# Six q tiles turned in 32x32 squares through DRAM on VectorE, and the routing table's lane one-hots as Sign steps on ScalarE

## The chip, the cores and the metric

The kernel runs on one core of a Trainium2 chip. A core has a matrix engine (TensorE), three engines for elementwise work (VectorE, ScalarE, GpSimd), a queue engine that issues DMAs (SyncE), an on-chip memory of 128 partitions and a small accumulator memory (PSUM) into which TensorE writes. Each engine works through its own instructions in the order in which the program gives them and waits on semaphores for the others. The metric is the device time of one execution in microseconds (us); less is better.

## What is computed

The kernel adds three things: the input x, a linear attention block, and a mixture of experts, both on the normalised x. S = 2048 tokens, D = 512, 32 heads of 16, 8 experts of which each token takes two, with 1792 hidden units. Cut to what matters here:

```python
def _A_ref(x, wqkv, wo):
    q, k, v = qkv[0], qkv[1], qkv[2]              # (b, heads, s, 16)
    phi = lambda t: jnp.where(t > 0, t + 1, jnp.exp(t)) + 1e-6
    pq, pk = phi(q), phi(k)
    kv = jnp.einsum("bhsd,bhse->bhde", pk, v)
    z = jnp.einsum("bhsd->bhd", pk)
    num = jnp.einsum("bhqd,bhde->bhqe", pq, kv)
    den = jnp.einsum("bhqd,bhd->bhq", pq, z)[..., None] + 1e-6
    return (num / den).transpose(...).reshape(B, S, D) @ wo

def _B_ref(x, w_gate, w1, w2):
    topk_idx = jnp.argsort(-(xf @ w_gate), axis=-1)[:, :2]
    gates = softmax(topk_val)
    for e in range(8):
        out = out + w_e * (silu(xf @ w1[e]) @ w2[e])   # w_e: the token's gate for e, or 0

xn = _layernorm(x)
return x + _A_ref(xn, A_wqkv, A_wo) + _B_ref(xn, B_w_gate, B_w1, B_w2)
```

## The kernel before

Tokens are tiled by 128: 16 tiles. Products keep nearly full precision by splitting each operand into a high part (rounded by a ScalarE copy, `split_hi`, L141) and a low part (the rest, a VectorE subtraction, `split_lo`, L144), and adding three products (high by high, high by low, low by high). The order of all work is written out by hand from the line `tc.manual_schedule()` on: each engine executes its steps in the order in which the code calls them. Buffers come from pools with a fixed number of slots per tag: `ta` (tag "a", 11 slots), `um` and `tb` (tag "u", 20), `sm` (tag "s", 18), and the accumulator tags "acc" (4), "mm" (2) and "tr" (2).

The kernel has three stages. The first normalises x, projects k and gathers two sums over all tokens; from them comes one matrix M (512x512), held in high and low parts, which merges kv with wo. The second, the q loop (L1531), goes over the q tiles t: here the change lies. The third runs the experts, from about 194 us on; in it the last five q tiles are finished too.

One iteration t of the q loop issues, in this order:

- `o_out(t-4)`: VectorE adds the finished attention output to x (L1478), SyncE stores it;
- side steps: the generator `side_jobs` gives VectorE a piece of the routing (which token goes to which place of which expert) worth some 2.6 us. In iterations 7 to 10 the piece is `table(q)`, q = 0 to 3 (L639): it builds, for 512 assignments (token and choice), a lane one-hot (`ohl`, 128 places in a block, L645) and a block one-hot multiplied by the token number (`mvb`, L647, L650). The products of the one-hots, `table_mm(q)` (L655), add up to the table of tokens by place. In iteration 11 `table_end` (L663) makes index lists of it, with which GpSimd gathers the rows of the first expert (`gather1`);
- `q_den(t-1)`: VectorE sums z-weighted features to denominators (L1410);
- `fetch_w` in iterations 8 to 10: SyncE issues the first three expert weight loads;
- `q_proj(t)`: TensorE's twelve matmuls of q (L1376) into an accumulator bank, then `q_exp(t)`, three ScalarE steps (L1385 to L1387);
- the `late` steps of the iteration before, `table_mm` among them (the last one, `table_mm(3)`, at the end of iteration 10);
- `q_norm(t-1)`: VectorE makes the reciprocals (L1414, L1415), GpSimd multiplies (L1416);
- `q_feat(t)`: VectorE makes the features (`q_phi`, L1393), GpSimd multiplies them by z (L1397);
- `load_x(t-2)`: SyncE fetches x for a later `o_out`;
- `q_transp(t-2)`: TensorE turns the normalised tile by four 128x128 transposes into an accumulator bank (L1422), ScalarE makes the high part and VectorE the low part of the result, `pqT`;
- from iteration 11 on `plain_w`: high and low parts of the first expert's weights;
- `o_proj(t-3)`: TensorE's twelve matmuls of `pqT` with M (L1437).

For the last five tiles (NO = 11 to 15) another way is in place: `pz_out` stores the normalised tile to DRAM as it is, `pz_in` fetches it late in the third stage by four DMAs of 32 partitions each, so that 32-row groups land on the partitions where they are wanted, and `q_turn` transposes it in 32x32 squares, two VectorE instructions of 128x256 (L1454). `q_hi` and `q_lo` make the two parts.

## Time and profile before

| what | value |
|---|---|
| time, median of 3 runs | 826.91 us (826.82 to 826.97) |
| the profiled execution | 826.48 us |
| its span, first to last instruction | 824.8 us |
| granted TensorE clock | 1.00 throughout |
| VectorE busy | 679.6 us (82%) |
| ScalarE busy | 541.2 us (66%) |
| TensorE from o_proj(0) at 123.2 us to the first expert matmul | 70.6 us |

The profile is of one execution. Its times are microseconds from the first instruction; PE is TensorE's matmul row, PEld its weight loads, DVE VectorE, ACT ScalarE, POOL GpSimd, SPq and ACTq the queues from which SyncE and ScalarE issue DMAs. L1376 is line 1376 of the kernel before. In the view of instructions in order of time a row has start, duration, engine, line, operation, output and inputs, shape, count (consecutive like instructions are merged), and in brackets the idle time just before with the instruction that ended it. A matmul's duration includes its way through the array, so matmuls overlap: their rate is read from starts.

### The profile page before, as it was taken

The numbers are of one execution on the slowest core, as the hardware profiler recorded it, in microseconds if no ns is written. First come the engines' busy times: TensorE is split into PE (matmuls) and PEld (weight loads), VectorE is DVE, ScalarE is ACT, GpSimd is POOL, SyncE is SP. The second block draws the span as 40 slices with busy tenths as digits, with TensorE's granted clock in tenths as the row PEclk, the third lists the DMA queues.
The fourth block names the chain that finished last, engine by engine and source line by source line (L and its number), as shares of the span: only waits on it lengthen the run. The fifth ranks groups of instructions, "written<-read, shape, count | busy, mean of one in ns | idle before, by whom it ended". The sixth has DMA issues, their size and how long they took to land. (4 is left out here: it accounts for less than half of the span.)

```text
span 824.8 us, 15897 instructions
## 1 busy us (share of the span) xinstructions
PE 820.3 (99%) x5361; PEld 752.1 (91%) x5361; DVE 679.6 (82%) x1470; ACT 541.2 (66%) x1162; POOL 249.7 (30%) x335
## 2 busy tenths in 40 slices
PE   9999999999999999999999999999999999999998
PEld 8999888889999999999999999999999888888886
DVE  7788889999878887878888788789888987887851
ACT  5575364358666768766876777677768766776650
POOL 5543224375310136121803250443127030012002
PEclk9999999999999999999999999999999999999999
DMA  5752136354764565566557464756576573249507
GB/s 168 252 199 87 52 135 202 128 183 166 234 200 135 152 197 108 145 166 184 131 136 187 151 143 136 206 130 161 155 190 130 161 188 113 84 132 232 154 1 178
DMA packets 106874, 127.69 MB, mean 155 GB/s; under 512 B 15198, under 2 KB 69854, under 8 KB 106758
## 3 DMA queue, kind: packets, MB, share of 16 engines
q1 hardware_dynamic: 92902, 106.43, 42.7%
q0 software_dynamic: 12880, 18.66, 11.8%
q10 hardware_dynamic: 1008, 1.57, 0.5%
q8 instruction: 43, 0.70, 0.3%
q14 instruction: 41, 0.34, 0.1%
HBM read 93.95 MB, written 31.09 MB: 152 GB/s over the span
## 5 line engine op out<-in xcount | busy, mean ns | idle before, releaser
L1174 POOL DMA_INDIRECT out_dram<-yo,sidx x22 | 35.1, 1595 | 282.6 <-DVE yo L1169 260.4
L1174 POOL DMA_INDIRECT out_dram<-yu,L x47 | 78.0, 1659 | 85.9 <-ACT yu L1267 59.0
L144 DVE TENSOR_TENSOR h<-hs,h 128x576 fp32r<-128x576 f32 (+7 forms) x112 | 77.7, 694 | 5.7 <-ACT h L141 5.4
L141 ACT ACTIVATE h<-hs 128x576 fp32r<-128x576 f32 (+7 forms) x112 | 72.3, 646 | 3.2
L1324 ACT ACTIVATE hs<-px 128x276 f32<-128x276 f32 (+7 forms) x54 | 21.1, 390 | 58.7 <-PE px L1316 58.6
L1339 ACT ACTIVATE hs<-hs 128x276 f32<-128x276 f32 (+7 forms) x54 | 23.0, 426 | 46.5 <-DVE hs L1338 46.5
L1338 DVE TENSOR_TENSOR hs<-pz,hs 128x276 f32<-128x276 f32 (+7 forms) x54 | 23.3, 431 | 34.6 <-PE pz L1316 34.0
L1343 DVE TENSOR_TENSOR hs<-px,hs 128x276 f32<-128x276 f32 (+7 forms) x54 | 23.3, 432 | 33.7 <-PE px L1316 33.7
L1047 POOL DMA_INDIRECT xg<-xn_d,gidx x37 | 40.8, 1104 | 28.2 <-DMA xq<-xs_d 7.2
L437 PE MATMUL gacc<-pkhl,xnhl 128*128 128x512 f32 x192 | 47.9, 397 | 0.0
L437 PEld LDWEIGHTS gacc<-pkhl,xnhl 128*128 128x128 f32 x192 | 34.8, 188 | 6.8
L1173 POOL MEMSET spacer<- 1x1 f32 x69 | 38.4, 557 | 6.8 <-DVE ws_3l L144 6.8
L1349 DVE TENSOR_TENSOR hs<-py,hs 128x276 f32<-128x276 f32 (+7 forms) x54 | 23.0, 426 | 13.7 <-PE py L1316 13.4
L1344 ACT ACTIVATE hs<-hs 128x276 f32<-128x276 f32 (+7 forms) x54 | 22.8, 422 | 17.0 <-DVE hs L1343 15.8
L411 POOL TENSOR_TENSOR zz<-zz,pk 128x512 f32<-128x512 f32 x14 | 18.2, 1300 | 48.3 <-DVE L L404 48.3
L1385 ACT ACTIVATE e_q<-qp 128x512 f32<-128x512 f32 x16 | 9.6, 598 | 35.4 <-PE qp L1376 31.7
L1198 PE MATMUL y<-w_1h,h 128*128 128x512 f32 (+2 forms) x88 | 32.0, 394 | 0.0
L1198 PE MATMUL y<-w_5h,h 128*128 128x512 f32 (+2 forms) x88 | 32.0, 394 | 0.0
L1198 PE MATMUL y<-w_2h,h 128*128 128x512 f32 (+2 forms) x88 | 32.0, 393 | 0.0
L1198 PE MATMUL y<-w_3h,h 128*128 128x512 f32 (+2 forms) x88 | 32.0, 393 | 0.0
L1198 PE MATMUL y<-w_0h,h 128*128 128x512 f32 (+2 forms) x88 | 32.0, 393 | 0.0
L1198 PE MATMUL y<-w_4h,h 128*128 128x512 f32 (+2 forms) x88 | 31.7, 393 | 0.0
(563 smaller groups left out, 3152.8 us busy)
## 6 DMA issues: line engine op xcount, KB each, us to landing
wst<-in_B_w_dram SPq DMA_DIRECT2D x196, 128.0 KB
wst<-in_B_w_dram SPq DMA_DIRECT2D x37, 512.0 KB
zz<-in_B_w_dram SPq DMA_DIRECT2D x26, 512.0 KB
xs_d<-xg SPq DMA_DIRECT2D x117, 64.0 KB
xq<-xs_d SPq DMA_DIRECT2D x28, 256.0 KB
x<-in_A_x_dram SPq DMA_DIRECT2D x27, 256.0 KB
xn_d<-xn SPq DMA_DIRECT2D x16, 256.0 KB
xnT<-xn SPq DMA_DIRECT2D x11, 256.0 KB
```

The costliest lines, as they stand in the source:

```text
L141: A.activation(hi, src, AF.Copy)
L144: V.tensor_tensor(lo, src, raw(hi), op=ALU.subtract)
L437: T.matmul(gacc[d], xnhl[:, a, d * P:(d + 1) * P], pkhl[:, b, :], start=(t == 0 and i == 0), stop=(t == NT - 1 and i == 2))
L1047: G.indirect_dma_start(out=raw(t), out_offset=None, in_=xn_d, in_offset=IOA(ap=gidx[:, b:b + 1], axis=0))
L1173: G.memset(spacer, 0.0)
L1174: st = G.indirect_dma_start(out=rows, out_offset=IOA(ap=idx, axis=0), in_=src, in_offset=None, compute_op=ALU.add).ins
L1198: T.matmul(ya[r, d][:m], h[a][:, d * P:d * P + m], w[b][:, n % 2, :], start=(first and i == 0), stop=(last and i == 2))
L1338: V.tensor_tensor(c12, pz_, c12, op=ALU.add)
L1339: A.activation(c12, c12, AF.Silu)
L1343: V.tensor_tensor(c22, px, c22, op=ALU.add)
L1344: A.activation(c22, c22, AF.Silu)
L1349: V.tensor_tensor(c11, pz_, c11, op=ALU.add)
```

## The change

It has two parts, and a third that follows from the second.

Tiles 4 to 9 (`TURNED`) are no longer transposed on TensorE. `q_norm` writes such a tile with its columns regrouped (the 32-column groups of each quarter put together); in the next iteration `pz_out` stores it to DRAM right behind `q_norm`, and `pz_in` fetches it back by the four DMAs of 32 partitions, after `load_x`. One iteration later `q_turn`, `q_hi` and `q_lo` take the place of `q_transp`. The fetched and the turned tile lie in the two halves of one "u" buffer, the two parts in an "s" buffer as before.

The lane one-hot of `table(q)` was one VectorE comparison of 128x1024. Now ScalarE makes eight instructions of 128x128, each sign(lane - (i + 0.5)) for one column of assignments, with the lane as bias: +1 for the places i below the lane and -1 from the lane on, a step instead of a one-hot. The lanes are held in 4 bytes for that.

The products then give sums of steps, and the table is the difference of neighbouring rows, halved. So `table_steps` builds a difference matrix on GpSimd (in iteration 8), `table_split` splits the sums into a high part (ScalarE) and a low part (VectorE) at the end of iteration 10, and `table_diff` multiplies them by the matrix, two small matmuls, in the middle of `q_proj(11)`. `table_end` runs behind that, after `q_den(10)`, not ahead of it.

```diff
@@ -45,6 +45,7 @@
 PASSES = ((0, 0), (0, 1), (1, 0))
 ND = 5
 NO = NT - ND
+TURNED = range(4, NO - 1)
 NE = 12
 NP = NF // 2
 NPLAIN = 2
@@ -110,6 +111,7 @@
     M_d = tc.dram_tile((2, 2, P, SW), F32, name="M_d")
     pz_d = tc.dram_tile((ND * P, D), F32, name="pz_d")
     xs_d = tc.dram_tile((E * RB * P, D), F32, name="xs_d")
+    pq_d = tc.dram_tile((len(TURNED) * P, D), F32, name="pq_d")
     gate_d = tc.dram_tile((E, BLK, P), F32, name="gate_d")
     sx_d = tc.dram_tile((P, BLK), F32, name="sx_d")
 
@@ -238,6 +240,7 @@
         G.affine_select(out=bmask, in_=bmask, pattern=[[DH, 8], [0, DH]],
                         compare_op=ALU.is_ge, fill=0.0, base=DH - 1, channel_multiplier=-1)
         iota(i_lane, [[1, P]])
+        G.tensor_scalar(i_lane, i_lane, 0.5, None, op0=ALU.add)
         iota(i_blk, [[1, NB]])
         iota(i_ov, [[1, NOV]])
         iota(i_e8, [[0, NT], [1, E]], base=-E)
@@ -441,7 +444,7 @@
 
 
     rt = cst
-    lane_f = rt.tile([P, NT, 2], F16, name="lane_f")
+    lane_f = rt.tile([P, NT, 2], F32, name="lane_f")
     blk_f = rt.tile([P, NT, 2], F16, name="blk_f")
     ohr = rt.tile([P, E, E], F32, name="ohr")
     gate = rt.tile([P, OV0], F32, name="gate")
@@ -640,10 +643,10 @@
         ts = slice(4 * q, 4 * q + 4)
         ohl = ta(f"ohl{q}", 8 * P, F16).rearrange("p (a b) -> p a b", a=8)
         mvb = ta(f"mvb{q}", 8 * NB, F16).rearrange("p (a b) -> p a b", a=8)
-        la = lane_f[:, ts, :].rearrange("p t k -> p (t k)").unsqueeze(2)
+        la = lane_f[:, ts, :].rearrange("p t k -> p (t k)")
         bl = blk_f[:, ts, :].rearrange("p t k -> p (t k)").unsqueeze(2)
-        V.tensor_tensor(ohl, i_lane.unsqueeze(1).broadcast_to([P, 8, P]),
-                        la.broadcast_to([P, 8, P]), op=ALU.is_equal)
+        for i in range(8):
+            A.activation(ohl[:, i, :], i_lane, AF.Sign, bias=la[:, i:i + 1], scale=-1.0)
         V.tensor_tensor(mvb, i_blk.unsqueeze(1).broadcast_to([P, 8, NB]),
                         bl.broadcast_to([P, 8, NB]), op=ALU.is_equal)
         m4 = mvb.rearrange("p (t k) b -> p t (k b)", k=2)
@@ -651,6 +654,14 @@
         tabm[q] = (ohl, mvb)
 
     tabm = {}
+
+    def table_steps():
+        step, tabp[2] = ta("step", P), um("step_r")[:, :P]
+        G.memset(step, 0.0)
+        for base, v in ((0, -0.5), (-1, 0.5), (P - 1, -0.5)):
+            G.affine_select(out=step, in_=step, pattern=[[1, P]], compare_op=ALU.not_equal,
+                            fill=v, base=base, channel_multiplier=-1)
+        G.tensor_copy(tabp[2], step)
 
     def table_mm(q):
         if q == 0:
@@ -660,8 +671,18 @@
             T.matmul(tabp[0], ohl[:, i, :], mvb[:, i, :],
                      start=(q == 0 and i == 0), stop=(q == 3 and i == 7))
 
+    def table_split():
+        tab = wp.tile([P, 2, NB], F32, tag="tab", name="tab", bufs=1)
+        hl = um("tabhl")
+        tabp[1] = tab, hl[:, :NB], hl[:, NB:2 * NB]
+        split(*tabp[1][1:], tabp[0])
+
+    def table_diff():
+        for i in range(2):
+            T.matmul(tabp[0], tabp[2], tabp[1][1 + i], start=(i == 0), stop=(i == 1))
+
     def table_end():
-        tab = wp.tile([P, 2, NB], F32, tag="tab", name="tab", bufs=1)
+        tab = tabp[1][0]
         t1, em = tab[:, 0, :], tab[:, 1, :]
         V.tensor_copy(t1, tabp[0])
         V.tensor_scalar(gidx, t1, -1.0, 0.0, op0=ALU.add, op1=ALU.max)
@@ -677,9 +698,10 @@
         yield from routing()
         for q in range(4):
             table(q)
+            if q == 1:
+                table_steps()
             late.append(lambda q=q: table_mm(q))
             yield 9.0
-        table_end()
 
     marks = []
     side = side_jobs()
@@ -1365,13 +1387,15 @@
         Q.dma_start(out[S + i * P:S + (i + n) * P, :].rearrange("(a p) d -> p a d", p=P),
                     zt.unsqueeze(1).broadcast_to([P, n, D]))
 
-    pq, pz, pqT = {}, {}, {}
+    pq, pz, pzt, pqT = {}, {}, {}, {}
 
     eq = {}
 
-    def q_proj(t, act=True):
+    def q_proj(t, act=True, mid=None):
         qp = psm("mm", f"qp{t}")
         for kc in range(KC):
+            if mid and kc == 2:
+                mid()
             for i, (a, b) in enumerate(PASSES):
                 T.matmul(qp, xT(t, a, kc), wq_v[kc // 2][b][:, kc % 2, :],
                          start=(kc == 0 and i == 0), stop=(kc == KC - 1 and i == 2))
@@ -1413,8 +1437,11 @@
         den = dens.pop(t)
         V.tensor_scalar(den, den, 1e-6, None, op0=ALU.add)
         V.reciprocal(den, den)
-        G.tensor_tensor(heads(pz[t]), heads(pq[t]),
-                        den.unsqueeze(2).broadcast_to([P, H, DH]), op=ALU.mult)
+        out, src, den = heads(pz[t]), heads(pq[t]), den.unsqueeze(2).broadcast_to([P, H, DH])
+        if t in TURNED:
+            out = pz[t].rearrange("p (a k h d) -> p k a h d", a=4, k=KC, d=DH)
+            src, den = (ap.rearrange("p (k a h) d -> p k a h d", a=4, k=KC) for ap in (src, den))
+        G.tensor_tensor(out, src, den, op=ALU.mult)
 
     def q_transp(t):
         p = psm("tr", f"pqp{t}")
@@ -1437,24 +1464,32 @@
                     T.matmul(op, pqT[t][:, a, kc * P:(kc + 1) * P], M_v[kc // 2][b][:, kc % 2, cols],
                              start=(kc == 0 and i == 0), stop=(kc == KC - 1 and i == 2))
 
+    def rows_d(t):
+        return pq_d[(t - TURNED[0]) * P:(t - TURNED[0] + 1) * P, :] if t in TURNED else \
+            pz_d[(t - NO) * P:(t - NO + 1) * P, :]
+
     def pz_out(t):
-        Q.dma_start(pz_d[(t - NO) * P:(t - NO + 1) * P, :], pz.pop(t))
+        Q.dma_start(rows_d(t), pz.pop(t))
 
     def pz_in(t):
-        pz[t] = ta(f"pzr{t}")
-        rows = pz_d[(t - NO) * P:(t - NO + 1) * P, :].rearrange("(c j) (a f) -> a j c f", j=BLK, f=P)
+        if t in TURNED:
+            both = raw(tb(f"pzr{t}"))
+            pz[t], pzt[t] = both[:, :D], both[:, D:]
+        else:
+            pz[t] = ta(f"pzr{t}")
+        rows = rows_d(t).rearrange("(c j) (a f) -> a j c f", j=BLK, f=P)
         for a in range(4):
             Q.dma_start(pz[t][a * BLK:(a + 1) * BLK].rearrange("j (c f) -> j c f", f=P), rows[a])
 
     def q_turn(t):
         src = pz.pop(t).rearrange("p (c k i) -> p c k i", i=BLK, k=KC)
-        pz[t] = ta(f"pzt{t}")
+        pz[t] = pzt.pop(t) if t in TURNED else ta(f"pzt{t}")
         dst = pz[t].rearrange("p (k c j) -> p c k j", k=KC, j=BLK)
         for q in range(2):
             V.transpose(dst[:, :, 2 * q:2 * q + 2, :], src[:, :, 2 * q:2 * q + 2, :])
 
     def q_hi(t):
-        pqT[t] = tb(f"pqT{t}").rearrange("p (h c) -> p h c", h=2)
+        pqT[t] = (sm if t in TURNED else tb)(f"pqT{t}").rearrange("p (h c) -> p h c", h=2)
         split_hi(pqT[t][:, 0], pz[t])
 
     def q_lo(t):
@@ -1528,6 +1563,7 @@
     q_transp(1)
     q_feat(3)
 
+    done = []
     for t in range(OLAG + 1, NT - 2):
         if t < NO + OLAG:
             o_out(t - OLAG - 1)
@@ -1541,9 +1577,13 @@
         q_den(t - 1)
         if 8 <= t < 11:
             fetch_w()
-        q_proj(t)
+        diff = 1 in tabp and table_end not in done
+        q_proj(t, mid=table_diff if diff else None)
         for f in due:
             f()
+        if diff:
+            table_end()
+            done.append(table_end)
         if t in (11, 12):
             gather1(0, 2 * t - 22)
         if t == 12:
@@ -1551,20 +1591,29 @@
         if t == 13:
             gather1(0, 4)
         q_norm(t - 1)
-        if t > NO:
+        if t > NO or t - 1 in TURNED:
             pz_out(t - 1)
         q_feat(t)
         if t == 4:
             Q.dma_start(out[NO * P:S, :], x[NO * P:S, :])
         if t < NO + 2:
             load_x(t - 2)
-            q_transp(t - 2)
+            if t - 1 in TURNED:
+                pz_in(t - 1)
+            if t - 2 in TURNED:
+                q_turn(t - 2)
+                q_hi(t - 2)
+                q_lo(t - 2)
+            else:
+                q_transp(t - 2)
         if t >= 11:
             plain_w()
         if t - OLAG < NO - 1:
             o_proj(t - OLAG)
         while 3 in tabm:
             late.pop(0)()
+            if 3 not in tabm:
+                table_split()
         if t in (11, 12):
             gather1(0, 2 * t - 21)
 
```

## The prediction

> **What bounds the kernel now.** I read the page first, then the busy time by stretches of the q loop, then the loop's instructions in order of time, engine by engine. The page says that TensorE hardly rests:
>
> ```profile
> span 824.8 us, 15897 instructions
> ...
> PE 820.3 (99%) x5361; PEld 752.1 (91%) x5361; DVE 679.6 (82%) x1470; ACT 541.2 (66%) x1162; POOL 249.7 (30%) x335
> ```
>
> So an edit pays only if it shortens TensorE's own stream, and costs whatever makes TensorE wait. The edit lies in the loop over q tiles (iterations t = 6 to 11). One iteration there, from one o_proj to the next, in the view of busy time by stretches (columns: PE, weight loads, DVE, ACT, POOL, granted clock):
>
> ```profile
> 153.61:159.83 6.22, 6.22 (x40) 5.07 (x38) 6.12 (x10) 2.46 (x5) 2.43 (x3) 1.00 0.52 171
> ```
>
> TensorE is full, but VectorE is busy 6.12 of 6.22 us too: two engines run at the same rate, and ScalarE is the free one. TensorE's instructions in order of time:
>
> ```profile
> 147.02 0.60 PE L1422 MATMUL pqp<-ident_r,pz 128*128 128x128 f32 x4
> 147.38 0.48 PE L1437 MATMUL op<-M0h,pqT 128*128 128x512 f32 x1
> ...
> 150.23 0.39 PE L1376 MATMUL qp<-wq0h,xnT 128*128 128x512 f32 x1
> ...
> 152.96 0.43 PE L660 MATMUL tabp<-mvb,ohl 128*128 128x66 f16 x8
> 153.22 0.63 PE L1422 MATMUL pqp<-ident_r,pz 128*128 128x128 f32 x4
> 153.61 0.48 PE L1437 MATMUL op<-M0h,pqT 128*128 128x512 f32 x1
> ...
> 166.02 0.48 PE L1437 MATMUL op<-M0h,pqT 128*128 128x512 f32 x1
> ...
> 169.13 0.48 PE L1376 MATMUL qp<-wq0h,xnT 128*128 128x512 f32 x1
> ...
> 172.34 0.48 PE L1437 MATMUL op<-M0h,pqT 128*128 128x512 f32 x1
> ...
> 175.19 0.39 PE L1376 MATMUL qp<-wq0h,xnT 128*128 128x512 f32 x1
> ```
>
> These are o_proj(4) at 147.38, q_proj(8) at 150.23, o_proj(5) at 153.61, o_proj(7) at 166.02, o_proj(8) at 172.34, q_proj(12) at 175.19. Twelve matmuls of 512 columns take 2.73 us (150.23 to 152.96), or 2.85 behind transposes; the table's eight take 0.26; the four transposes 0.36 to 0.39. Three iterations, o_proj(4) to o_proj(7), take 18.64 us, 6.21 each. VectorE's part of an iteration:
>
> ```profile
> 145.54 0.63 DVE L1393 SCALAR_TENSOR_TENSOR pq<-qp,e_q 128x512 f32<-128x512 f32 x1
> 146.09 0.68 DVE L144 TENSOR_TENSOR pqT<-pqp,pqT 128x512 fp32r<-128x512 f32 x1
> 146.68 0.68 DVE L1478 TENSOR_TENSOR x<-op,x 128x512 f32<-128x512 f32 x1
> 147.28 1.88 DVE L645 TENSOR_TENSOR ohl<-i_lane,lane_f 128x1024 f16<-128x1024 f16 x1
> 149.08 0.70 DVE L647 TENSOR_TENSOR mvb<-i_blk,blk_f 128x528 f16<-128x528 f16 x1
> ...
> 150.44 0.68 DVE L1410 TENSOR_REDUCE den<-pz 128x32 f32<-128x512 f32 x1
> 151.15 0.18 DVE L1414 TENSOR_SCALAR den<-den 128x32 f32<-128x32 f32 x1
> ...
> 151.64 0.63 DVE L1393 SCALAR_TENSOR_TENSOR pq<-qp,e_q 128x512 f32<-128x512 f32 x1
> ```
>
> Starts follow each other by less than a duration, so I take starts: q_phi 0.55, low part 0.60, o_out 0.60, lane one-hot 1.80, block table 1.36, q_den 0.71, denominator 0.49: 6.1 us, with no wait. ScalarE does its four steps and then idles until the next q_proj:
>
> ```profile
> 147.22 0.60 ACT L1385 ACTIVATE e_q<-qp 128x512 f32<-128x512 f32 x1 [3.46 <-PE qp L1376]
> 147.85 0.63 ACT L1386 ACTIVATE e_q<-e_q 128x512 f32<-128x512 f32 x1
> 148.52 0.72 ACT L1387 ACTIVATE e_q<-e_q,eps 128x512 f32<-128x512 f32 x1
> 149.15 0.58 ACT L141 ACTIVATE pqT<-pqp 128x512 fp32r<-128x512 f32 x1
> ```
>
> q_exp, from its start to its last end: 2.02 us. The low part of tile 4 ends at 146.77, and o_proj(4) reads it from about 147.9: VectorE is about one microsecond ahead of need. This spare is what the change spends.
>
> **The change part by part.**
>
> *TensorE, removed.* Six groups of four transposes: about 0.48 each in the three iterations without table matmuls just ahead (0.36 and the 0.12 by which the next group is slower), 0.39 in the other three: 2.6 us. Added: table_diff, two products of 66 columns. Eight such take 0.26, but these have 4-byte weights; between 0.1 and 0.6 I take 0.4. If nothing waited, the kernel would gain 2.2.
>
> *The durations of what comes in.* VectorE's turn of a tile, Sign by the nearest shape on ScalarE (128x128 with a per-partition operand), and the high part from SBUF:
>
> ```profile
> 756.17 0.76 DVE L1454 STREAM_TRANSPOSE pzt<-pzr 128x256 f32<-128x256 f32 x2
> ```
>
> ```profile
> 313.27 1.26 ACT L1267 ACTIVATE yu<-yu,gu 128x128 f32<-128x128 f32 x4
> ...
> 782.83 0.63 ACT L141 ACTIVATE ws_6h<-wr 128x512 fp32r<-128x512 f32 x1
> 783.35 0.63 ACT L141 ACTIVATE pqT<-pzt 128x512 fp32r<-128x512 f32 x1
> ```
>
> Turn: 0.77. Eight Signs: four in 1.26 make 0.29 each, 2.35 in all (bounds: a quarter of the 0.6 of 512 columns, 0.15, and no overlap, 0.39). High part: 0.52 to the next start, 0.62 to its end. A handoff between engines: 0.04.
>
> *A new wait on VectorE, each iteration.* Before, TensorE turned the tile early and VectorE found its high part ready. Now q_turn is VectorE's own step, q_hi on ScalarE follows it, and q_lo stands next in VectorE's queue: it waits 0.04 + 0.62 + 0.04 = 0.70 there, with o_out, the table and q_den behind it. VectorE's iteration: 6.1 - 1.80 + 0.77 + 0.70 = 5.8, no shorter than TensorE's 2.73 + 2.73 + 0.36 = 5.8.
>
> *A loop through ScalarE.* In program order ScalarE does q_hi, then the next table's eight Signs, then q_exp, on which q_phi waits, then q_turn, on which the next q_hi waits: 0.52 + 2.35 + 2.02 + 0.55 + 0.77 + three handoffs 0.12 = **6.33 us per iteration**, whatever TensorE does. That alone takes the place of the 6.21.
>
> *A loop through DRAM.* The tile is normalised on GpSimd, stored, fetched back by four DMAs (SP waits for the store to land), and turned an iteration later:
>
> ```profile
> 139.92 1.06 POOL L1416 TENSOR_TENSOR pz<-pq,den 128x512 f32<-128x512 f32 x1 [4.35 <-DVE den L1415]
> ...
> 151.86 1.06 POOL L1416 TENSOR_TENSOR pz<-pq,den 128x512 f32<-128x512 f32 x1 [3.79 <-DVE den L1415]
> ```
>
> ```profile
> 0.83 0.86 SPq L155 DMA_DIRECT2D x<-in_A_x_dram  x2
> ...
> 740.45 1.89 SPq L1447 DMA_DIRECT2D pzr<-pz_d  x4
> ...
> 818.90 3.59 ACTq L1480 DMA_DIRECT2D out_dram<-xo  x4
> ```
>
> ```profile
> 3.49 0.69 DVE L273 BATCH_NORM_STATS2 bs<-x 128x6 f32<-128x512 f32 x1 [1.80 <-DMA x<-in_A_x_dram]
> ```
>
> Issue to landing is at most 2.66 (first load, 0.83 to 3.49) and at most 2.65 (last store, issued at 822.15, span end 824.8); both hold something beside the transfer, so I take 2.45 for store and fetch. The last of four fetches is issued 1.42 after the first. From one denominator to the next but one: denominator step 0.71, normalising 1.06, store 2.45, fetch 1.42 + 2.45, handoffs 0.12; then q_turn 0.77, wait 0.70, q_lo 0.60, o_out 0.60, table 1.36, q_den 0.71: 12.95 for two iterations, **6.48 each**. It is the longer loop while a landing is over 2.3.
> The Trainium skill, "DMA: Bandwidth & Descriptors", section on the anatomy of a GpSimd-issued DMA, fits 2.0 us plus bytes over 436 GB/s: 2.6 for the store, 2.15 for a 64 KB fetch; by it the sum below would be 4.5 instead of 5.0. The rows here are upper ends, and no run shows a single landing.
>
> *The sum, at the places where TensorE waits.* Iteration 6: tile 4 is normalised at 140.98, stored by 143.47, its last fetch lands at 147.38 (q_phi(6) left VectorE free at 146.09); turn, high part, and o_proj(4) starts at 148.9 instead of 147.38: +1.5. Iterations 7 to 9: 3 x 6.48 = 19.43 instead of 18.64: +0.8. Iteration 11: table_diff stands in the middle of q_proj(11), ahead of o_proj(8). Its operand is split on VectorE behind q_lo(8):
>
> ```profile
> 171.63 0.22 DVE L666 COPY tab<-tabp 128x66 f32<-128x66 f32 x1
> ```
>
> So after o_proj(7): 6.48 until tile 8's high part, 0.60 q_lo, 0.22 + 0.04 for the split, 0.4 table_diff, 1.37 second half of q_proj(11): 9.1 until o_proj(8) instead of 6.32: +2.8. Then q_proj(12) follows by 2.73 instead of 2.85: -0.1. **In all +5.0**, and from q_proj(12) on I see TensorE full as before, so it stays: VectorE has waits of its own from 180 us, and gathers and weights shift along.
>
> *Costed at nothing.* table_steps: five small GpSimd steps, covered by the 3.79 idle ahead of the normalising in the row at 151.86; uncovered, its excess over that would delay one tile. The rearranged output of q_norm: 1.06 as before (up to 0.2 more costs 0.1 per iteration). table_end now behind q_den: its gathers have some 4 us until x_block. SP is held about 4 us per iteration by the fetch behind its store; o_out's stores and three weight loads queue behind, but their buffers are needed two or more iterations later. table_diff's half us is counted.
>
> **The rivals.**
> 1. *Faster.* VectorE and ScalarE stay ahead, TensorE's sum counts: -2.2, 824.7 us. It decides if both loops are under TensorE's 5.8. For it: 1.8 us leave VectorE, ScalarE is idle 3.5 per iteration. Against it: the queues' order. 14%.
> 2. *No change.* Landings well under 2.3 and Signs near 0.2 bring the loops to some 5.6, under TensorE's 5.8: +0.3 in iteration 6 (turn and high part without a DMA wait), 3 x (5.9 - 6.21) = -0.9, and some 1.4 of iteration 11's wait: +0.8, 827.7. For it: nothing in the trace is a bare landing. Against it: the four scaled activations are the very shape. 13%.
> 3. *Slower, more: DMA contention.* A fetch issued ahead of three weight loads landed late:
>
> ```profile
> 213.71 0.34 SPq L1117 DMA_DIRECT2D xq<-xs_d  x1
> ```
>
> ```profile
> 219.92 0.77 DVE L1126 STREAM_TRANSPOSE xr<-xq 128x256 f32<-128x256 f32 x2 [0.79 <-DMA xq<-xs_d]
> ```
>
> Weights are fetched in iterations 8 to 10. Landings of 3.2 instead of 2.45 add 1.5 + 3 x 0.75 + 0.75 = 4.5: 836.4. 12%.
> 4. *Table loads.* Sign appears nowhere in the trace before. The trace loads ScalarE's table twice, ahead of the first Relu/Exp/Copy work and ahead of Silu:
>
> ```profile
> L141 ACT ACT_TABLE_LOAD x1 | 1.3, 1283 | 0.8 <-PEq L1769 0.8
> L1296 ACT ACT_TABLE_LOAD x1 | 1.3, 1283 | 0.0
> ```
>
> If Sign is not in the loaded table, each of four iterations gets two loads in ScalarE's loop: 4 x 2.57 = 10.3 more, 842. Relu, Exp, Identity and Copy share one here, so 3%.
> The Trainium skill, "ScalarE: Activation LUTs", section on table sets as the hidden batching unit, says that cheap functions are in every set and a foreign one costs a load each way; it does not name Sign there. The load's 1283 ns agrees with these rows.
>
> **How the numbers follow.** The profiled execution took 826.48 us, 1.68 more than its span; 824.8 + 5.0 + 1.68 = 831.5; the median of the runs, 826.91, lies 0.43 above that execution, so I forecast **831.9**, with 58%; its own range is 830.1 (no DMA wait at all, only ScalarE's loop: 0.3 + 3 x 0.12 + 2.65 - 0.1 = 3.2) to 834 (landings of 2.8: each 0.1 us of landing adds 0.2 + 0.3 + 0.1). With rivals 3 and 4 slower has 73%, no change 13%, faster 14%; a change under 0.2% (1.65 us) is about what can't be told from none. Left out of the range are rival 1 and rival 4: 826.5 to 837.5.
>
> **What would show it.** Right: in the profile after, VectorE's low part of pqT waits some 0.7 on ScalarE's pqT each iteration; q_turn waits on a DMA at tile 4; the q loop's period is 6.3 to 6.5; TensorE's wait before table_diff is over 2 us; nothing differs after q_proj(12) but the offset. Wrong: o_proj groups under 6 us apart, or a Sign over 0.4 us, or TensorE idle later than q_proj(12).

## The result and the profile after

The changed kernel takes 837.08 us (median of 4 runs, 835.74 to 838.03) against 826.92 in the same session; the ratio is 1.0122, 95% interval 1.0104 to 1.0139. The forecast was 831.9, with 834 as the top of its own range. The profiled execution of the changed kernel is the lowest of its four, 835.74, so the trace explains 9.2 us of span; the median lies 1.3 above it.

The page's first lines of the changed kernel: TensorE's busy share falls by a point, and the span grows.

```profile
span 834.0 us, 15961 instructions
...
PE 821.5 (98%) x5339; PEld 750.1 (90%) x5339; DVE 676.1 (81%) x1479; ACT 551.0 (66%) x1195; POOL 253.8 (30%) x341
```

TensorE in order of time, at the places that the prediction names (start, duration, ..., in brackets the idle time before and what ended it):

```profile
148.28 0.50 PE L1464 MATMUL op<-M0h,pqT 128*128 128x512 f32 x1 [1.31 <-ACT pqT L143]
...
151.48 0.39 PE L1400 MATMUL qp<-wq0h,xnT 128*128 128x512 f32 x1
...
154.69 0.50 PE L1464 MATMUL op<-M0h,pqT 128*128 128x512 f32 x1
...
168.81 0.50 PE L1464 MATMUL op<-M0h,pqT 128*128 128x512 f32 x1 [1.53 <-ACT pqT L143]
...
172.19 0.48 PE L1400 MATMUL qp<-wq0h,xnT 128*128 128x512 f32 x1
...
177.64 0.38 PE L682 MATMUL tabp<-tabhl,step_r 128*128 128x66 f32 x2 [3.82 <-DVE tabhl L146]
...
179.68 0.63 PE L1464 MATMUL op<-M0h,pqT 128*128 128x512 f32 x1
...
183.68 0.39 PE L1400 MATMUL qp<-wq0h,xnT 128*128 128x512 f32 x1
...
202.69 0.42 PE L1316 MATMUL hp<-xB,w_0h 128*128 128x288 f32 x2
```

These are o_proj(4), q_proj(8), o_proj(5), o_proj(7), q_proj(11), table_diff, o_proj(8), q_proj(12) and the first expert matmul. q_proj(7), just ahead of the first turned tile, starts 0.22 us earlier than before (144.08 against 144.30), so the loss by place is the offset plus 0.22:

| from q_proj(7) to | lost so far | in this step |
|---|---|---|
| o_proj(4) | 1.1 | 1.1 |
| o_proj(7) | 3.0 | 1.9 |
| o_proj(8) | 7.6 | 4.6 |
| q_proj(12) | 8.7 | 1.1 |
| first expert matmul (193.79 before) | 9.1 | 0.4 |

After that the offset stays: 8.90 at the first expert matmul, 9.2 at the end. Nearly all of the loss, 8.7 of 9.1, lies in some 40 us. Its two large steps are iteration 9 (o_proj(7)) and iteration 11. VectorE's rows there show who was late:

```profile
146.79 0.77 DVE L1489 STREAM_TRANSPOSE pzr<-pzr 128x256 f32<-128x256 f32 x2 [0.23 <-DMA pzr<-pq_d]
...
160.97 0.69 DVE L146 TENSOR_TENSOR pqT<-pzr,pqT 128x512 fp32r<-128x512 f32 x1 [0.70 <-ACT pqT L143]
...
167.32 0.77 DVE L1489 STREAM_TRANSPOSE pzr<-pzr 128x256 f32<-128x256 f32 x2 [1.41 <-DMA pzr<-pq_d]
...
175.20 0.77 DVE L1489 STREAM_TRANSPOSE pzr<-pzr 128x256 f32<-128x256 f32 x2 [1.49 <-DMA pzr<-pq_d]
```

The turns of tiles 4, 7 and 8 wait for their fetch, those of 5 and 6 don't; each low part waits 0.70 for the high part. SyncE's queue shows why tiles 7 and 8 differ from the others (a fetch is issued as soon as its store has landed):

```profile
153.39 0.34 SPq L1472 DMA_DIRECT2D pq_d<-pz  x1
...
155.46 1.74 SPq L1482 DMA_DIRECT2D pzr<-pq_d  x4
...
158.77 0.43 SPq L955 DMA_DIRECT2D wst<-in_B_w_dram  x1
159.69 0.35 SPq L1472 DMA_DIRECT2D pq_d<-pz  x1
...
163.50 2.21 SPq L1482 DMA_DIRECT2D pzr<-pq_d  x4
...
166.39 0.41 SPq L955 DMA_DIRECT2D wst<-in_B_w_dram  x1
166.84 0.56 SPq L1472 DMA_DIRECT2D pq_d<-pz  x1
...
171.86 1.74 SPq L1482 DMA_DIRECT2D pzr<-pq_d  x4
```

The store of tile 6 lands 2.07 us after its issue. That of tile 7, issued 0.92 behind a 512 KB weight load, needs 3.81, and that of tile 8, 0.45 behind one, 5.02. The third load stands 0.46 ahead of tile 9's store, which needs 4.41 (174.72 to 179.13); its turn at 182.62 doesn't wait, since VectorE itself is late by then. Last, the busy time by stretches (PE, weight loads, DVE, ACT, POOL, granted clock) for the first half of q_proj(11) with the wait, the rest of it, and o_proj(8):

```profile
172.19:177.64 5.45, 1.63 (x12) 1.06 (x9) 2.84 (x8) 1.51 (x4) 2.28 (x2) 1.00 0.70 178
177.64:179.68 2.04, 2.04 (x8) 1.68 (x9) 1.94 (x9) 0.00 (x0) 0.00 (x0) 0.81 0.77 295
179.68:183.68 4.00, 4.00 (x14) 3.18 (x13) 1.70 (x4) 2.21 (x4) 3.22 (x3) 0.67 0.66 151
```

o_proj(8) takes 4.00 us instead of 2.85: the granted clock is 0.67 there. Nothing in the prediction foresaw that.

### The profile page after: what moved, and what is told of

Read it like the earlier page. It is cut to its first block, busy times and chain, and to the rows that moved or that the text cites. A ratio compares the mean times of both kernels' runs of the same rounds, so it can differ in the third digit from the quotient of the medians.

```text
span 834.0 us, 15961 instructions
## 1 busy us (share of the span) xinstructions
PE 821.5 (98%) x5339; PEld 750.1 (90%) x5339; DVE 676.1 (81%) x1479; ACT 551.0 (66%) x1195; POOL 253.8 (30%) x341
## 5 line engine op out<-in xcount | busy, mean ns | idle before, releaser
L1346 ACT ACTIVATE hs<-px 128x276 f32<-128x276 f32 (+7 forms) x54 | 21.0, 390 | 58.4 <-PE px L1338 58.3
L1356 ACT ACTIVATE hs<-px 128x276 f32<-128x276 f32 (+7 forms) x54 | 21.1, 391 | 16.2 <-PE px L1338 14.8
```

## The experiments

The theory after reading the trace has four parts: (a) the two new chains, ScalarE's loop and the wait of 0.70, set a period of 6.3; (b) stores of turned tiles land late because weight loads are queued just ahead of them; (c) table_diff holds TensorE because its operand stands behind a tile that waits for DRAM; (d) the matmuls behind that wait run at half rate because TensorE had been idle. The rivals: the Sign steps themselves cost the time; the landings are late for the turn's own traffic; a wait taken away from one place only shows at the next. Diffs below are against the changed kernel and cut to the lines that matter. All times are medians beside the kernel before on the same chip (826.48 to 827.04 in the sessions). The changed kernel was timed in one session only, and the runs of one kernel spread over up to 4 us (e15's over 7), so a difference of about 1 us between two of these medians decides nothing; the places in the traces are read beside them.

| run | us | ratio, 95% interval | first expert matmul at |
|---|---|---|---|
| before | 826.92 | | 193.79 |
| changed | 837.08 | 1.0104 to 1.0139 | 202.69 |
| e1, turn only | 837.68 | 1.0115 to 1.0149 | 204.67 |
| e2, Sign only | 826.85 | 0.9993 to 1.0013 | 193.94 |
| e3, loads behind the fetch | 836.73 | 1.0111 to 1.0145 | 203.22 |
| e5, loads in iteration 5 | 837.03 | 1.0112 to 1.0145 | 204.54 |
| e9, loads out of the way | 834.07 | 1.0074 to 1.0112 | 200.83 |
| e12, loads on ScalarE's queue | 836.05 | 1.0092 to 1.0125 | 203.01 |
| e4, table_diff late | 844.90 | 1.0204 to 1.0238 | 211.23 |
| e6, split first | 835.97 | 1.0095 to 1.0132 | 203.90 |
| e13, TensorE kept busy | 837.94 | 1.0119 to 1.0153 | 202.79 |
| e7, high parts held | 835.58 | 1.0100 to 1.0134 | 201.54 |
| e8, e7 and loads in iteration 5 | 834.29 | 1.0077 to 1.0110 | 201.38 |
| e10, e7 and loads out of the way | 830.46 | 1.0032 to 1.0065 | 196.33 |
| e17, e10 held from tile 6 on | 831.14 | 1.0035 to 1.0068 | 198.46 |
| e11, e10 with o_proj later | 833.15 | 1.0056 to 1.0090 | 200.11 |
| e15, e11 and q_den later | 834.72 | 1.0065 to 1.0128 | 201.71 |
| e16, e11 reordered | 836.66 | 1.0095 to 1.0132 | 204.72 |

### Each part alone

```diff
 e2:
-TURNED = range(4, NO - 1)
+TURNED = range(0)
```

> Only the Sign steps with the difference matrix; every tile turned on TensorE as in the kernel before. Theory: VectorE loses 1.8 us per iteration, ScalarE's 2.4 fit into its 3.5 idle, the split no longer stands behind a tile that waits for DRAM, so table_diff waits under 0.5 and costs 0.4 itself: 0.4 to 0.9 above the kernel before, 827.3 to 827.8. Rival (the Sign steps in ScalarE's queue, or the split and the difference in the middle of q_proj(11), cost by themselves): table_diff waits over 2 us and the time is 830 or more.

826.85, no difference from before. TensorE's table rows and ScalarE's loop in it:

```profile
168.78 0.43 PE L670 MATMUL tabp<-mvb,ohl 128*128 128x66 f16 x8
...
170.51 0.30 PE L681 MATMUL tabp<-tabhl,step_r 128*128 128x66 f32 x2
```

```profile
149.54 2.44 ACT L648 ACTIVATE ohl<-i_lane,lane_f 128x128 f16<-128x128 f16 x8
153.06 0.60 ACT L1408 ACTIVATE e_q<-qp 128x512 f32<-128x512 f32 x1 [1.09 <-PE qp L1399]
```

table_diff starts without any wait, and ScalarE still idles 1.09 us ahead of q_exp: the Sign steps, the split and the difference cost nothing that can be measured while the tiles are turned on TensorE. The rival "Sign costs" falls. But the 1.1 us that each iteration frees on VectorE gains nothing either: TensorE was full.

```diff
 e1:
-        for i in range(8):
-            A.activation(ohl[:, i, :], i_lane, AF.Sign, bias=la[:, i:i + 1], scale=-1.0)
+        V.tensor_tensor(ohl, i_lane.unsqueeze(1).broadcast_to([P, 8, P]),
+                        la.broadcast_to([P, 8, P]), op=ALU.is_equal)
...
-            if q == 1:
-                table_steps()
...
+        table_end()
```

> Only the turn through DRAM; the lane one-hots, the table and its index lists as in the kernel before. Theory (queue order and late landings): VectorE keeps the comparison of 1.80 and gets the turn of 0.77 and the wait of 0.70, 6.1 + 1.5 = 7.6 us per iteration against TensorE's 6.2, in the iterations that build the table; so about 1.4 us in each of four iterations besides 0.9 in iteration 6, and nothing waits for a split in iteration 11: 6 us above the kernel before, 833. The waits of the turn on a DMA should all but vanish, since VectorE itself comes later. Rival (the stores delayed behind the weight loads set the pace whatever VectorE does): waits on a DMA of about 1.4 at tiles 7 and 8 as in the changed kernel, 836 or more. Rival (ScalarE's Sign steps are what costs): under 829.

837.68: as slow as both parts together, and above what was expected. o_proj(4), o_proj(5) and o_proj(6) are 6.9 and 7.3 apart (148.39, 155.31, 162.59): VectorE is the bound there, with no idle but the 0.70. The waits of the turn at tiles 7 and 8 fall to 0.61 and 0.79, so from there on VectorE's order and the late stores share the pace; the expected 6 us are there at q_proj(12) (181.45 against 175.19). The rest came behind it, not foreseen: tile 9's turn waits 3.51 for its fetch and the gathered rows come late.

```profile
169.08 0.77 DVE L1487 STREAM_TRANSPOSE pzr<-pzr 128x256 f32<-128x256 f32 x2 [0.61 <-DMA pzr<-pq_d]
...
185.72 0.77 DVE L1487 STREAM_TRANSPOSE pzr<-pzr 128x256 f32<-128x256 f32 x2 [3.51 <-DMA pzr<-pq_d]
```

So the turn alone is enough for the whole loss. Beside the turn the Sign part is not free: it shortens the iterations (6.3 from o_proj(5) to o_proj(6) instead of 7.3), and the wait of table_diff, which stands behind the turn, costs more than that: q_proj(12) is 8.5 late in the changed kernel and 6.3 late here.

### The loads ahead of the stores

```diff
 e3:
-        if 8 <= t < 11:
-            fetch_w()
...
             if t - 1 in TURNED:
                 pz_in(t - 1)
+            if 8 <= t < 11:
+                fetch_w()
 e5, instead:
+        for _ in range(3 if t == 5 else 0):
+            fetch_w()
 e9, instead (two at the end of iteration 4, one in iteration 11):
+            if t == 4:
+                fetch_w()
+                fetch_w()
...
+            if t == 11:
+                fetch_w()
```

> The changed kernel with the weight loads of iterations 8 to 10 issued behind the fetch of the turned tile instead of ahead of its store. Theory (the stores landed 3.8 to 5.0 us after their issue because 512 KB were queued 0.4 to 0.9 us ahead of them): stores land in about 2.0 again, the turn's waits of 1.41 and 1.49 fall under 0.3, iterations 7 to 9 give 1 us back and iteration 11 some 1.5, and with the idle before table_diff down to some 2.3 us TensorE may keep its rate (1.6 more): 2.5 to 4.5 below the changed kernel, 832.5 to 834.5. Rival (the landings are late for the turn's own traffic, or ScalarE's loop of 6.3 sets the period anyway): within 1 us of 837.

836.73, no change, but not for the rival's reason. SyncE waits for the store's landing ahead of the fetch, so a load behind the fetch comes only 1.04 ahead of the next store (165.43 and 166.47): that store's fetch starts at 170.99, 4.5 later. The place in the program moved, the place in time didn't.

> The changed kernel with its first three expert weight loads all issued at the start of iteration 5, some 5 us ahead of the first store of a turned tile, instead of one in each of iterations 8, 9 and 10. Theory (a store lands in 2.0 us alone and in 3.8 to 5.0 us behind a 512 KB load): all six stores land in about 2.0 to 2.2, the turn waits on no DMA but at tile 4 (0.2), ScalarE's loop of 6.3 to 6.4 us sets the period up to o_proj(7); the idle before table_diff is 2.3 or less, with little or no half rate behind it: 3 to 5 below the changed kernel, 832 to 834. Rival (the late landings come from the traffic of the turn itself): landings of 4 to 5 stay, within 1 us of 837.

837.03, again the same, and again a misplaced load. SyncE issued the loads behind two small stores of the routing (137.31 and 137.70), at 139.16 and later:

```profile
139.16 1.00 SPq L955 DMA_DIRECT2D wst<-in_B_w_dram  x2
140.35 0.37 SPq L961 DMA_DIRECT2D wst<-in_B_w_dram  x1
141.46 0.35 SPq L1472 DMA_DIRECT2D pq_d<-pz  x1
...
146.78 1.76 SPq L1482 DMA_DIRECT2D pzr<-pq_d  x4
...
163.79 0.34 SPq L1472 DMA_DIRECT2D pq_d<-pz  x1
...
165.85 1.75 SPq L1482 DMA_DIRECT2D pzr<-pq_d  x4
```

With three loads ahead, tile 4's store takes 5.3 us; with none, tile 7's takes 2.06. TensorE idles 5.44 ahead of o_proj(4) here, and afterwards the high parts of tiles 5 to 8 come 6.3, 6.3, 7.0 and 6.3 apart. The delay went where the loads went.

> The changed kernel with its first expert weight loads where no store of a turned tile follows them closely: two at the end of iteration 4 (some 8 us ahead of the first store; in the run before this the place in iteration 5 came only 2 us ahead of it), the third in iteration 11 behind the last fetch. All other order as in the changed kernel. Theory (late landings come from loads just ahead on the queue): all six stores land in about 2.0, o_proj(4) is at 147 to 148.5, the high parts follow each other by ScalarE's loop of 6.3 (one of 7.0 where the difference matrix is built on GpSimd), table_diff waits about 2 us without half rate behind it, o_proj(8) is at about 176 and q_proj(12) 3 to 4 us later than in the kernel before: 831.5 to 833, 4 to 5.5 below the changed kernel. Rival (landings are late for another reason): 836 or more.

834.07, 3.0 below the changed kernel; in the traces q_proj(12) comes 2.6 earlier (181.05 against 183.68). All six stores land in 2.0 to 2.1, tile 8's for one:

```profile
166.30 0.34 SPq L1472 DMA_DIRECT2D pq_d<-pz  x1
...
168.31 1.75 SPq L1482 DMA_DIRECT2D pzr<-pq_d  x4
```

Of the turns only tile 4's waits (0.49); the others follow each other by 6.31, 6.52 and 6.32. The rival, the turn's own traffic, falls, since that traffic is the same here. This confirms (b), and (a): with late landings gone, ScalarE's loop is the longer one. It is 1 to 2.6 us short of what was expected, since half rate followed the wait for the table here too (below).

```diff
 e12:
-            fetch_w()
+            fetch_w(A)
...
```

> The changed kernel with the three weight loads of iterations 8 to 10 issued from ScalarE's queue at the same place of the program instead of SyncE's. This asks whether a store lands late because the load stands ahead of it in the same queue, or because both use the same transfer engines. If the queue's order does it: landings near 2.0 at tiles 7 to 9, waits of the turn under 0.4 and 3 to 5 us below the changed kernel, 832 to 834, less some half us that ScalarE spends on issuing. If the shared engines do it: landings of 3 to 5 stay, 836 to 838.

836.05. The stores land in 2.0 (158.91 to 160.93, 166.51 to 168.52), but the turn still waits, now for the fetch:

```profile
159.96 0.77 DVE L1490 STREAM_TRANSPOSE pzr<-pzr 128x256 f32<-128x256 f32 x2 [1.14 <-DMA pzr<-pq_d]
...
167.03 0.77 DVE L1490 STREAM_TRANSPOSE pzr<-pzr 128x256 f32<-128x256 f32 x2 [0.67 <-DMA pzr<-pq_d]
```

Here the first load went out at 154.72, and the fetch issued from 154.80 to 156.54 was there only at 159.96. The same happened to the next two: in ScalarE's order the loads went out at 154.72, 160.95 and 168.00, each beside a fetch and more than 4 us ahead of a store. So a load delays a transfer that stands beside it on another queue too; the shared engines do at least part of it. Whether the order within one queue adds to it for the stores stays open, since no store stood near a load here.

### The wait for the table, and the half rate behind it

```diff
 e4 (table_diff, table_end and the first gather behind o_proj(8)):
-        q_proj(t, mid=table_diff if diff else None)
+        q_proj(t)
...
             o_proj(t - OLAG)
+        if diff:
+            table_diff()
+            table_end()
...
```

> The changed kernel with table_diff and table_end moved from the middle of q_proj(11) to the end of iteration 11, behind o_proj(8); the first gather follows there. Theory (TensorE's queue stands behind table_diff for 3.8 us, and the half rate after it costs 1.6): o_proj(8) starts once the high part of tile 8 is there, some 2.3 us earlier, the idle ahead of it is about 2 us, no matmuls at half rate follow: 3 to 4.5 below the changed kernel, 832.5 to 834, less up to 1 if the gathers come too late for the transposes of iteration 12. Rival (o_proj(8) waits for the same tile, so the stall only moves and the half rate follows it all the same): 1 us or less below 837.

844.90, a miss by 11 us in the other direction. Up to q_proj(12) it went as expected (179.78, 3.9 earlier than in the changed kernel). But table_end now stood on VectorE behind the turn of tile 9, which waited 2.92 for its fetch, and the gathers behind that:

```profile
176.54 0.50 PE L1464 MATMUL op<-M0h,pqT 128*128 128x512 f32 x1 [1.59 <-ACT pqT L143]
179.64 0.30 PE L682 MATMUL tabp<-tabhl,step_r 128*128 128x66 f32 x2
...
193.23 0.72 PE L1115 MATMUL xep<-ident_r,xg 128*128 128x128 f32 x4 [10.43 <-DMA xg<-xn_d,gidx]
```

The index list is made at 186.41, against 178.85 in the changed kernel and 171.89 before. The table's way to the gathers is a deadline of its own.

```diff
 e6 (behind o_proj, the table products and their split):
-            if t - 2 in TURNED:
+            if t - 2 not in TURNED:
+                q_transp(t - 2)
+            elif t != 10:
                 q_turn(t - 2)
...
+        if t == 10:
+            q_turn(8)
+            q_hi(8)
+            q_lo(8)
```

> The changed kernel with the steps of iteration 10 in another order: o_proj(7), the last table products and their split come ahead of the turn, high part and low part of tile 8, weight loads where they were. Theory (table_diff waits only because its operand is split behind a turn that waits for DRAM): table_diff finds its operand and costs its 0.4 alone; o_proj(8) waits some 2 us for tile 8 itself, no matmuls at half rate: 2.5 to 4 below the changed kernel, 833 to 834.5. Rival (the wait for tile 8 is the cost and only changes its place): 1 us or less below.

835.97. The mechanism is as expected, table_diff waits 0.16 and o_proj(8) 0.67, and q_proj(12) comes 3.8 earlier (179.87). The gain is nearly all given back: the index list is made at 178.76, where it was, because table_end still stands behind tile 8 on VectorE. TensorE waits 1.42 for gathered rows in iteration 12, and matmuls at half rate follow there (o_proj(9) takes 4.7). So (c) explains where TensorE waits, and the rival is right about the time: the wait moved to the gathers.

```diff
 e13 (ahead of table_diff's two matmuls):
+        wt = psm("tr", "keep")
+        for _ in range(14):
+            T.matmul(wt, xT(11, 0, 0), wq_v[0][0][:, 0, :], start=True, stop=True)
```

> The changed kernel with fourteen matmuls of 512 columns (about 3.2 us) put on TensorE just ahead of table_diff, into an accumulator bank that nobody reads; they change no output. Theory (the matmuls behind the wait ran at half rate because TensorE had been idle for 3.8 us): the wait before table_diff falls to 0.7 or less, q_proj(11)'s second half takes 1.4 and o_proj(8) 2.8 instead of 2.0 and 4.0, and 1.4 to 1.8 us come back: about 835.4. Rival (those matmuls were slow because they waited for tile 8's parts): nothing changes, 837.

TensorE's rows, and the clock of the second half of q_proj(11) and of o_proj(8):

```profile
174.19 3.33 PE L683 MATMUL keep<-wq0h,xnT 128*128 128x512 f32 x14
178.50 0.38 PE L685 MATMUL tabp<-tabhl,step_r 128*128 128x66 f32 x2 [0.98 <-DVE tabhl L146]
```

```profile
178.50:180.20 1.70, 1.70 (x9) 1.43 (x9) 1.63 (x6) 0.00 (x0) 0.00 (x0) 1.00 0.90 346
180.20:182.93 2.73, 2.73 (x13) 2.25 (x12) 1.08 (x5) 1.95 (x3) 2.06 (x2) 1.00 0.45 106
```

The clock stays at 1.00, o_proj(8) takes 2.73 instead of 4.00. Its operands were as late as before (178.50 against 177.64), so idleness made the half rate, not late operands: (d) holds. The time didn't follow: 837.94, no gain. In the profiled execution table_diff's operand came 0.9 later, q_proj(12) only 0.75 earlier, and the first expert matmul where it was (202.79).

### The order of high and low parts

```diff
 e7:
             if t - 2 in TURNED:
                 q_turn(t - 2)
-                q_hi(t - 2)
-                q_lo(t - 2)
+                if t == 6:
+                    q_hi(4)
+                    q_lo(4)
...
+        if 8 <= t <= 12:
+            q_hi(t - 3)
+            q_lo(t - 3)
         q_den(t - 1)
```

> The changed kernel with the high and low parts of tiles 5 to 9 moved to the next iteration, behind the table's steps and ahead of q_den: VectorE has o_out and the block table between a turn and its low part, ScalarE makes the Sign steps ahead of the high part, and the split of iteration 10 comes ahead of tile 8's high part. Weight loads where they were. Theory: VectorE's wait of 0.70 goes, ScalarE's loop falls from 6.3 to 5.0, table_diff does not wait; the waits of the turn on late landings at tiles 7 to 9 stay: 3 to 5 below the changed kernel, 832 to 834. Rival (the order on VectorE and ScalarE is not what costs; only the landings are): 836 to 837.

> Both: high and low parts held to the next iteration, and the weight loads in iteration 5. Theory: no loop is longer than TensorE's own 5.8 to 5.9 us per iteration; iteration 6 keeps its 0.5 to 1, the rest gives back 2 to 2.5 against the kernel before: 825 to 827. Rival (the loop through DRAM stays the longer one at a landing of 2.0 each way): periods of 6.2 and more, 829 or more.

> As the run before in this call, and the high and low parts of tiles 5 to 9 held to the next iteration, behind the table's steps. Theory: all loops are under TensorE's own 5.8 to 5.9 us, table_diff waits for nothing, and what is left is the first turned tile (0.5 to 1.3) and gathers that come up to half a microsecond late: q_proj(12) at or before its place in the kernel before, 826 to 828. Rival (TensorE's removed transposes show in full): 824.5 to 825.5. Rival (another loop takes over): 829 or more.

e7 takes 835.58, between what its theory and its rival expected. As its theory says, table_diff waits for nothing, but o_proj(7) waits 1.19 and 1.14 for its two parts, and half rate follows there (a clock of 0.59 from 170.5 to 174.0); the 1.5 below the changed kernel lie within the spread of the two (834.43 to 837.80 against 835.74 to 838.03). e8 fails for the reason of e5 (tile 4 late, 5.86 of idle). e10, with the loads truly out of the way, takes 830.46, 6.6 below the changed kernel and still 3.8 above the kernel before. TensorE's waits in it:

```profile
148.20 0.50 PE L1464 MATMUL op<-M0h,pqT 128*128 128x512 f32 x1 [1.43 <-ACT pqT L143]
155.30 0.50 PE L1464 MATMUL op<-M0h,pqT 128*128 128x512 f32 x1 [0.80 <-ACT pqT L143]
156.55 0.73 PE L1464 MATMUL op<-M0h,pqT 128*128 128x512 f32 x2 [0.52 <-DVE pqT L146]
...
180.41 0.51 PE L1115 MATMUL xep<-ident_r,xg 128*128 128x128 f32 x4 [0.75 <-DMA xg<-xn_d,gidx]
```

From o_proj(6) to q_proj(12) TensorE waits for nothing, and o_proj(6) to o_proj(7) takes 5.92 against 6.19 before: the removed transposes do show. They are worth less than what the first two turned tiles and the gathers cost. q_proj(12) is 1.6 late, the first expert matmul 2.5; the last 1.3 us of the span arise among the experts: from their first matmul to the end e10 takes 632.3 us, the kernel before 631.0 and all other runs but e16 between that and 631.8. Why stays open.

### Four attempts to hide the rest

e11 puts o_proj(4) to o_proj(8) one iteration later on TensorE, e15 adds q_den behind table_end, e16 moves the table's steps and x's loads so that e11's waits go, and e17 is e10 held from tile 6 on, with e15's q_den.

> High and low parts held, weight loads out of the way (as in the run that had both), and on TensorE o_proj(4) to o_proj(8) one iteration later: iteration 7 has no o_proj, iterations 8 to 11 have o_proj(t-4), iteration 12 has o_proj(8) and o_proj(9); o_out follows. Theory (what is left there is a delay, not a rate: the first turned tile is ready 1.2 us late and tile 5 waits 1.3 behind the Sign steps): TensorE has 2.8 us more before it needs each tile and waits for none, so its removed transposes show: 824.5 to 826. Rival (the delay only moves to the end of the loop, to the table or the gathers): 828 or more.

> The same, and in iteration 11 q_den behind table_end, so that the gathers start some 0.6 us earlier. Theory: if the gathers of the first expert are what ends last, 0.3 to 0.7 below the run before in this call; if TensorE is full there, the same time.

> The run with o_proj one iteration later lost what it gained to three new waits: table products ahead of VectorE's block one-hots (1.34 and 2.75), a store of a turned tile's fetch held 1.9 by the load of x in front of it, and the split behind the turn of tile 8 (1.44). Here the table products stand behind o_proj, the last ones with their split and the difference in iteration 11 around o_proj(7), the load of x behind the fetch, and the first transposes of gathered rows behind o_proj(9). Theory (all that remains are delays that the order can hide): TensorE waits under 1.5 in all between o_proj(3) and the experts, 824.5 to 827. Rival (VectorE, ScalarE and the way through DRAM together need as long as TensorE did before, and the wait only moves again): 829 or more.

> The version with loads out of the way and high and low parts held, but held from tile 6 on only (tile 5 keeps its place ahead of the Sign steps), and q_den behind table_end in iteration 11. Theory (0.8 and 0.5 that TensorE waited for tile 5's parts, and 0.75 for a late gather, are part of the 3.8 that remained): 1 to 2 us below that version, 828.5 to 829.5. Rival (tile 5's wait only moves to the next tile): 830 to 831.

All four are slower than e10, or level with it (e17), and all are slower than the kernel before. e15's runs lie between 831.25 and 838.42, so its question against e11 stays open. Each took its wait away and met another. In e11 SyncE's queue stands 1.92 at the load of x (159.17), ahead of tile 7's fetch. In e16 ScalarE idles 5.98 ahead of the Sign steps at 167.96, and the view names the store of a finished tile as what ended that. In e17 tile 5's wait moves to tile 6 (0.83 and 0.46), as its rival said, and VectorE's turn of tile 7 waits 2.25 for its fetch:

```profile
166.39 0.77 DVE L1489 STREAM_TRANSPOSE pzr<-pzr 128x256 f32<-128x256 f32 x2 [2.25 <-DMA pzr<-pq_d]
```

By that row the fetch was there 3.4 us after its last issue (162.98), against 1.6 for the turns of tiles 7 and 8 in the changed kernel, and no weight load was issued between 140 and 178 in e17. So, if the view names the right wait, weight loads are not the only thing that makes a landing late; what else does stays open.

Whether some other order would make the change pay stays open; none of the seventeen kernels is faster than the one before.

## Why the prediction was right and wrong

The side was right (slower, 73%), the size was half: 5.0 forecast, 9.1 in the trace by the first expert matmul, and a median 3.1 above the top of the range. Two steps of the sum failed: it took one landing time for all six tiles, and it had no term for the half rate behind a long wait. By place:

- **Iteration 6, +1.5**: 1.1 at o_proj(4), 1.5 by q_proj(8), since the third matmul waits for the low part as well. Right, but in part by two errors that cancel: the landing was shorter (2.0 instead of 2.45), and the low part's wait had been left out.
- **Iterations 7 to 9, 3 x 6.48 = +0.8**: +1.9. The loop through DRAM was named the longer one "while a landing is over 2.3". Alone a landing takes 2.0, so ScalarE's loop of 6.33 counts where no load is near: 6.31 from o_proj(5) to o_proj(6), and 6.32 between turns in e9. Behind a load it takes 3.8, and iteration 9 took 7.8. The step that failed is the one landing time of 2.45 for all six tiles: too long for a tile alone, too short behind a load. The page of the Trainium skill that the prediction named, "DMA: Bandwidth & Descriptors" (anatomy of a GpSimd-issued DMA), gives 2.6 for the store, by an estimate from its fit; issued from SyncE's queue, with no weight load near, it took 2.0 here.
- **Rival 3, contention, 836.4 at 12%**: its mechanism is what happened, and e9 prices it at 3.0 in the medians (2.6 in the traces at q_proj(12)). That 836.4 lies near the measured time is in part luck: it counted 4.5 for late landings at every tile, and half rate, which it didn't have, made up the rest. Its evidence was in the trace before, a fetch that came 0.79 late near weight loads, and the loads of iterations 8 to 10 stand next to the new stores in the code. "o_out's stores and three weight loads queue behind" looked only at what comes behind the fetch, not at what is ahead of the next store.
- **Iteration 11, +2.8**: 4.6, of which the late landing of tile 8 is 1.5 and half rate 0.4 (the stretch from table_diff to o_proj(8) took 2.04, in e12, at full rate, 1.68). Place and cause, table_diff behind the split behind q_lo(8), were right; table_diff waited 3.82, "over 2 us".
- **o_proj(8) to q_proj(12), -0.1**: +1.1, the half rate: o_proj(8) took 4.00, and 2.73 in e13, where the clock stayed at 1.00. This is the second step that failed: no step of the prediction asked what an idle of four microseconds does to the matmuls behind it.
- **"table_end now behind q_den: its gathers have some 4 us"**: the stretch behind q_proj(12) took 0.4 more, 0.26 of it a wait for gathered rows, and in e4, e6 and e10 they are what is late next.
- **Signs at 0.29, 2.35 for eight; no table load**: 2.44, no load. Right. table_diff's two products, taken at 0.4, took 0.22. The wait of 0.70 on each low part: measured 0.69 to 0.70.
- **"If nothing waited", -2.2**: never reached. In e10's clean iteration 0.27 show where 0.39 to 0.48 was counted.

Once q_proj(12) is past, nothing but the offset changes, as forecast, save for the gathers (0.26 of idle at 199.53).

## What to carry to other kernels

Before a tile is sent through DRAM on a tuned path, list what stands ahead of its store in the same queue and what else moves at that time: an unhurried bulk load costs nothing until something urgent stands behind it, and moving it in the program moves it in time only if the queue isn't waiting there. Time freed on an engine that isn't the bound is worth nothing by itself (e2); whether it is a condition of the better orders here isn't shown, since no run held the parts back or moved the loads without the Sign steps. A wait that is taken away is worth only the distance to the next one: read the next deadline (here the index list for the gathers) before moving work past it.

## What the runs showed of the hardware

**Half rate comes in stretches of 3.4 us, and an idle of 1.7 can be enough.** In e9 TensorE idled 2.18, ran the next matmuls at full rate, and then at half:

```profile
175.03 0.38 PE L682 MATMUL tabp<-tabhl,step_r 128*128 128x66 f32 x2 [2.18 <-DVE tabhl L146]
...
175.56 0.40 PE L1400 MATMUL qp<-wq1l,xnT 128*128 128x512 f32 x1
...
176.41 0.63 PE L1400 MATMUL qp<-wq1l,xnT 128*128 128x512 f32 x1
...
179.67 0.40 PE L1464 MATMUL op<-M1h,pqT 128*128 128x512 f32 x1
```

From about 176.0 to 179.4 the matmuls start 0.43 apart instead of 0.23, at a granted clock of 0.51. In the changed kernel the stretch is about 178.9 to 182.3, after 3.82 of idle. In e12 one followed an idle of 1.72 ahead of the experts:

```profile
198.25 0.51 PE L1116 MATMUL xep<-ident_r,xg 128*128 128x128 f32 x4 [1.72 <-DMA xg<-xn_d,gidx]
```

The o_proj behind it took 4.42 (198.59 to 203.01). Yet e12 idled 2.73 ahead of table_diff and kept its rate, as e5 did with 1.96, so the length of the gap alone doesn't decide. The Trainium skill, "TensorE: Matmul & The Clock Gate", Part 1, describes a window of about 3.4 us that runs freely, after whose idle turn the rate is halved; the lengths of the stretches here agree. A free phase could explain why 1.72 and 2.18 did it and 2.73 didn't, but only if a window that is idle in part is enough; no run tests that. Its rule in "HAM oscillation", no idle gap over about 3.4 us, would let all of these gaps but the 3.82 pass; the runs measure otherwise.

**VectorE slows beside GpSimd.** The lane one-hot took 1.88 in the kernel before, where GpSimd's multiplication overlapped it by some 0.8 us (146.79, 1.28 long), and 1.21 in e1, where GpSimd was idle; in e2 the block table that then stood beside GpSimd took 1.36 instead of 0.70 (1.38 and 1.31 in the next two iterations; in the fourth, with an overlap of 0.1, 0.70):

```profile
147.22 1.36 DVE L649 TENSOR_TENSOR mvb<-i_blk,blk_f 128x528 f16<-128x528 f16 x1
```

So in e2 taking the one-hot off VectorE freed 1.1 us in such an iteration, not 1.8: the other 0.7 goes to whatever of this kind stands beside GpSimd. The Trainium skill, "SBUF — State Buffer", "Who interferes with whom", says that a VectorE instruction with two inputs in this memory and a GpSimd instruction that reads it exclude each other; the 0.7 more, with 0.8 of overlap, agrees. This was read from rows, not tested by a run of its own.
